# Weights streamed for a seven-product multiplication: one fetch for two products instead of one each

## The chip, the cores and the metric

The program runs on one core of one Trainium2 chip. The metric is the device time of one execution in microseconds (us). TensorE (PE) multiplies, VectorE (DVE) and ScalarE (ACT) do the elementwise work, GpSimd (POOL) and SyncE (SP) mostly start transfers. All transfers share the core's 16 DMA engines; those that SP, ACT and POOL start go through queues of their own, called q1, q10 and q0 in the profile.

## The reference

A retention layer is followed by two feed-forward layers over 3072 tokens. All arrays are float32.

```python
for t in range(S):                       # 4 batches, 8 heads, 768 steps, head width 64
    state = gamma * state + k[t] outer v[t]
    y[t] = (q[t] @ state) / 8
x = y as (3072, 512)
h = x @ moe_w_in                         # (512, 2048)
x = (h * sigmoid(1.702 * h)) @ moe_w_out # (2048, 512)
h = x @ moe2_w_in
r = maximum(h, 0)
return (r * r) @ moe2_w_out
```

## The kernel before

Every float32 factor is split into a high and a low part (hi, lo), and a product is lo·hi + hi·hi + hi·lo: three matmuls of 128x128 by 128x512 in place of one.

**Stages.** The retention layer comes first (lines 403 to 564). Then the first feed-forward layer runs on blocks 0 to 3 of 512 tokens in the plain way, with all its weights in SBUF (`up` and `down`, lines 577 to 615). While this goes on, a background program, the `maker`, builds the operands of a faster scheme out of the weights, on ACT and DVE, and writes them to DRAM through POOL and SP. The last stage, from `up2` and `down2` on, uses that scheme: a multiplication of 2x2 blocks that needs seven products instead of eight. It handles 1024 tokens at a time: one such double block of the first layer, named (0, 2), then three of the second layer, (1, 0), (1, 1) and (1, 2).

**The seven products.** `PRODUCT[i]` names the weight operand and the activation operand of product i. In `up2` a round p (0 to 7) handles one 128-row slice of each half of the hidden layer. A product there is six matmuls that read one weight operand, hi and lo together 2 KB in each of the 128 partitions, 256 KB in all. Products add up in PSUM banks X, Y and Z, and `copy` on ACT and `add` on DVE bring them into the tiles `g`. Round p runs product 1 of p, then 4 and 3 of round p-1, then 2, 6, 5 and 7 of p. In `down2` the products follow `ORDER` = 1, 2, 6, 5, 7, 4, 3, each in four slices m; one slice is twelve matmuls on two operands (p = 2m and 2m+1).

**The stream of operands.** The second stage's weights don't fit in SBUF. Each operand is a row `kw[l][m][p][i]` in DRAM (l the layer, m = 0 for up and 1 for down), 256 KB in one piece, 2 KB for each partition. `queue` lists the operands in the order of use. `fetch` starts the next transfer on SP into one of `SLOTS` = 8 places of 2 KB per partition; two of them exist early, six take the memory of the first layer's tiles `gs`, `gh` and `gl`. A transfer into a place waits until the matmuls that read its last content are through:

```python
while queue and len(fetched) < SLOTS:
    ...
    nc.sync.dma_start(out=t.bitcast(F32), in_=kw[l][m][p][PRODUCT[i][0]])
```

**What else moves data then.** At the start of round 4 of each double block `loads()` has POOL fetch the next double block's activations: four transfers `xb` of 512 KB. `background(BGUP)`, called twice a round, gives the maker 1.8 us of DVE work; one of its jobs reads 512 KB (`raw`, on ACT's queue, line 233) and writes 896 KB (`wq`, on POOL's queue, line 302, in pieces of 1 KB). The maker ends inside (1, 0). Every engine runs its instructions in the order in which the program was written; a transfer's start waits in the order of the engine that starts it.

Of the kernel before, what the change touches and what calls it, by code (L numbers as in the profile page):

```python
# [10 lines left out]
F32 = mybir.dt.float32  # L11
# [7 lines left out]
P = 128  # L19
# [18 lines left out]
QS = (11, 12, 21, 22)  # L38
PAD = 96
NSTD = 4  # L40
SLOTS = 8
EARLY = 2
BG = 4.8
BGUP = 1.8

A11, A12, A22, S1, S2, S3, S4 = range(7)
B11, B21, B22, T1, T2, T3, T4 = range(7)  # L50
PRODUCT = {1: (A11, B11), 2: (A12, B21), 3: (S4, B22), 4: (A22, T4), 5: (S1, T1), 6: (S2, T2), 7: (S3, T3)}

# [2 lines left out]
def tile_retention_then_two_ffns(  # L55
# [136 lines left out]
    def weights(f, s):  # L192
        while (f, s) not in ws:
# [5 lines left out]

    jobs = [(m, i) for m in range(2) for i in range(NJ)]  # L200

    kw = [
        [
            [dr_p.tile([7, P, 2, 256], F32, tag=f"kw{l}{m}{p}", name=f"kw{l}{m}{p}") for p in range(NQ)]
            for m in range(2)
        ]
        for l in range(2)
    ]
    made = set()
    acts = deque()  # L210

# [23 lines left out]
    def make_first():  # L235

        load(0)
        load(1)
        with tc.tile_pool(name="k1", bufs=2, side="right", reuse_waits="tile") as pool:

            def low(m, p, t, h, done):
                while not done:
                    yield None
                v.tensor_tensor(out=h[:, :, :, 1], in0=t, in1=h[:, :, :, 0], op=ALU.subtract)
                nc.gpsimd.dma_start(
                    out=kw[0][m][p][S1:S4 + 1].rearrange("i p k c -> p i (k c)"),
                    in_=h.bitcast(F32).rearrange("p i k h c -> p i (k h c)"),
                )
                made.add((0, m, p))
                yield 1.25  # L250

            last = None
            for m in range(2):
                for p in range(NQ):
                    w0, w1 = ws[p, m], ws[NQ + p, m]

                    dst = kw[0][m][p].rearrange("i p k c -> p i (k c)")
                    f0, f1 = (w.bitcast(F32).rearrange("p (j k) h c -> p j (k h c)", j=2) for w in (w0, w1))
                    if m == 0:
                        nc.sync.dma_start(out=dst[:, A11:A12 + 1], in_=f0)  # L260
                        nc.sync.dma_start(out=dst[:, A22], in_=f1[:, 1])
                    else:
                        nc.sync.dma_start(out=dst[:, A11], in_=f0[:, 0])
                        nc.sync.dma_start(out=dst[:, A12:A22 + 1], in_=f1)
                    w = pool.tile([P, 8, P], F32, tag="w", name=f"wf_{m}_{p}", bufs=1)
                    v.tensor_tensor(out=w[:, 0:4], in0=w0[:, :, 0], in1=w0[:, :, 1], op=ALU.add)
                    yield 0.7
                    v.tensor_tensor(out=w[:, 4:8], in0=w1[:, :, 0], in1=w1[:, :, 1], op=ALU.add)
                    yield 0.7
                    q0, q1, q2, q3 = (w[:, 2 * k:2 * k + 2] for k in range(4))  # L270
                    a11, a12, a21, a22 = (q0, q1, q2, q3) if m == 0 else (q0, q2, q1, q3)
                    t = pool.tile([P, 4, 2, P], F32, tag="t", name=f"wt_{m}_{p}")
                    s1, s2, s3, s4 = (t[:, k] for k in range(4))
                    v.tensor_tensor(out=s1, in0=a21, in1=a22, op=ALU.add)
                    v.tensor_tensor(out=s3, in0=a11, in1=a21, op=ALU.subtract)
                    yield 0.85
                    if last is not None:
                        yield from low(*last)
                    v.tensor_tensor(out=s2, in0=s1, in1=a11, op=ALU.subtract)
                    v.tensor_tensor(out=s4, in0=a12, in1=s2, op=ALU.subtract)  # L280
                    h = pool.tile([P, 4, 2, 2, P], F32R, tag="h", name=f"wh_{m}_{p}")
                    done = later(lambda t=t, h=h: nc.scalar.copy(out=h[:, :, :, 0], in_=t))
                    last = m, p, t, h, done
                    yield 0.85
            yield from low(*last)

    def make_second():

        with tc.tile_pool(name="k2", bufs=2, side="right", reuse_waits="tile") as pool:
# [7 lines left out]
            def low(n, w, t, done):  # L297
                while not done:
                    yield None
                m, i = jobs[n]  # L300
                v.tensor_tensor(out=t[:, :, 1], in0=w[:, 1:8], in1=t[:, :, 0], op=ALU.subtract)
                nc.gpsimd.dma_start(
                    out=kw[1][m][i // 2][:, :, i % 2].rearrange("i p c -> p i c"),
                    in_=t.bitcast(F32).rearrange("p i h c -> p i (h c)"),
                )
                if i % 2:
                    made.add((1, m, i // 2))
                yield 1.1
# [3 lines left out]
            for n in range(len(jobs)):  # L312
# [26 lines left out]
                    yield from low(*last)  # L339
                v.tensor_tensor(out=wf, in0=wf, in1=hm, op=ALU.add)  # L340
                yield 0.7
                a21, a11, a12, a22, s1, s2, s3, s4 = (w[:, k] for k in range(8))
                v.tensor_tensor(out=s1, in0=a21, in1=a22, op=ALU.add)
                v.tensor_tensor(out=s3, in0=a11, in1=a21, op=ALU.subtract)
                yield 0.6
# [54 lines left out]
    with tc.manual_schedule():  # L400
# [277 lines left out]
        for l, n in blocks:  # L678
            first, *rest = [(i, m) for i in ORDER for m in range(NQ // 2)]
            for p in range(NQ + 1):  # L680
                if p < NQ:
                    queue.append((l, n, 0, 1, p))
                else:
                    queue.extend((l, n, 1, first[0], q) for q in range(2))
                if p > 0:
                    queue.extend((l, n, 0, i, p - 1) for i in (4, 3))
                if p < NQ:
                    queue.extend((l, n, 0, i, p) for i in (2, 6, 5, 7))
            for i, m in rest:
                queue.extend((l, n, 1, i, p) for p in (2 * m, 2 * m + 1))  # L690
        fetched = {}
        turn = [0]

        def fetch():
            while queue and len(fetched) < SLOTS:
                l, n, m, i, p = key = queue[0]
                if turn[0] % SLOTS >= len(wr_p):
                    return
                assert key[:1] + key[2:3] + key[4:] in made
                queue.popleft()  # L700
                t = wr_p[turn[0] % SLOTS].tile([P, 2, 256], F32R, tag="w", name="r{}_{}_{}_{}_{}".format(*key))
                turn[0] += 1
                nc.sync.dma_start(out=t.bitcast(F32), in_=kw[l][m][p][PRODUCT[i][0]])
                fetched[key] = t

        gen = iter(())
        for n in range(NSTD):
# [50 lines left out]
        def up2(l, n, first, loads):  # L758
# [3 lines left out]

            def product(i, p, a, start):
                s, b = PRODUCT[i]
                w = fetched.pop((l, n, 0, i, p)).rearrange("p k (h c) -> p k h c", h=2)
                for k in range(2):
                    hi, lo = w[:, k, 0], w[:, k, 1]
                    matmul(a, lo, xh[b][:, k], start and k == 0, False)
                    matmul(a, hi, xh[b][:, k], False, False)
                    matmul(a, hi, xl[b][:, k], False, k == 1)  # L770
                fetch()

            def gt(q, p):
                return g[q, p // 2][:, p % 2]

            def copy(t, a):
                nc.scalar.copy(out=t, in_=a)  # L777
                while late:
                    late.popleft()()
# [8 lines left out]
            for p in range(NQ + 1):  # L788
                if p == NQ // 2:
                    loads()  # L790
                if p < NQ:
                    xb[p] = bank(f"X{l}_{n}_{p}")
                    product(1, p, xb[p][0], True)
                    copy(gt(11, p), xb[p][0])
                else:
                    next(first)
                if p > 0:
# [13 lines left out]
                    if p == NQ - 1:  # L811
                        prepare(l, n)
                if p < NQ:
                    if (l, n) != blocks[-1] and p < NQ - 1:
                        background(BGUP)
                    yb = bank(f"Y{l}_{n}_{p}")
                    product(2, p, yb[0], True)
                    add(gt(11, p), yb[0])
                    banks.append(yb[1])
                    product(6, p, xb[p][0], False)  # L820
                    copy(gt(12, p), xb[p][0])
                    zb[p] = bank(f"Z{l}_{n}_{p}")
                    product(5, p, zb[p][0], True)
                    product(7, p, xb[p][0], False)
                    copy(gt(22, p), xb[p][0])
                    add(gt(22, p), zb[p][0])
                    if (l, n) != blocks[-1] and p < NQ - 1:
                        background(BGUP)
# [46 lines left out]
        def down2(l, n, tick):  # L875
# [40 lines left out]
            for i in ORDER:  # L916
# [6 lines left out]
                for m in range(NQ // 2):  # L923
# [8 lines left out]
                    for e in range(2):  # L932
                        a = acc[e][0]
                        for p in (2 * m, 2 * m + 1):
                            w = fetched[l, n, 1, i, p].rearrange("p j (h c) -> p j h c", h=2)
                            wh, wl = w[:, e, 0], w[:, e, 1]
                            s0, s1 = p == 0 and i in (1, 2, 5), p == NQ - 1
                            matmul(a, wl, hi[:, p % 2], s0, False)
# [1 line left out]
                            matmul(a, wh, lo[:, p % 2], False, s1)  # L940
                        if m == NQ // 2 - 1:
                            after(i, e, acc)
                    for p in (2 * m, 2 * m + 1):
                        del fetched[l, n, 1, i, p]
                    fetch()
                    yield
                if i == 2:
# [105 lines left out]
```

## Time and profile before

| what | value |
|---|---|
| three timed runs | 1071.35, 1073.38, 1073.88 us (median 1073.38) |
| span of the profiled execution, first to last instruction | 1070.7 us |
| PE busy | 1049.9 us, 98% |
| DVE, ACT, POOL busy | 796.5, 511.6, 95.0 us |
| DMA | 259.34 MB, 242 GB/s |
| SP's queue q1 | 156.64 MB, 45.2% of 16 engines |
| POOL's queue q0 | 83.89 MB, 21.3% |
| fetches `r<-kw` | 448 of 256 KB, 2.9 us from start to landing (median) |

The profiled execution's own time is its span of 1070.7 us; the timed runs lie 0.6 to 3.2 us above it and their median 2.7 us. Busy shares are averages over stages with different limits, so the stages have to be looked at one by one. A matmul's busy time overlaps the next one's, so PE's idle time is the span of a stretch less its busy time.

### The profile page before, as it was taken

What the parts mean: (1) busy time and instruction counts of PE and PEld (TensorE: products, weight loads), DVE (VectorE), ACT (ScalarE), POOL (GpSimd) and SP (SyncE); (2) the same over time, 40 slices, a digit from 0 to 9 for tenths busy, and PEclk for the clock granted to TensorE, in tenths of its full rate; (3) what the DMA queues carried; (4) which work ended last, traced back from release to release, by engine and by line L of the source; (5) the groups of instructions that cost most, each with busy time, mean ns of one, the idle gap of its engine ahead of it and who ended that gap; (6) DMA issues with size and microseconds to landing.
All of it is one profiled execution on the core that took longest, in us unless ns stands there. A gap on an engine that the chain in (4) does not pass through costs nothing.

```text
span 1070.7 us, 15321 instructions
## 1 busy us (share of the span) xinstructions
PE 1049.9 (98%) x5482; PEld 870.7 (81%) x5482; DVE 796.5 (74%) x1197; ACT 511.6 (48%) x862; POOL 95.0 (9%) x143
## 2 busy tenths in 40 slices
PE   8799999999999999999999999999999999999998
PEld 6788888888888888887888887888888888888886
DVE  4988897888698889855598587889345887345953
ACT  5787554433454545454546343455233465233443
POOL 3100110111111121101000001000100000000000
PEclk9999999999999999999999999999999999999999
DMA  9997677855467685599866799766876667766664
GB/s 331 339 330 275 249 247 255 318 191 191 180 223 248 202 323 189 172 360 317 299 208 204 247 295 326 238 216 210 290 213 193 194 210 230 219 193 192 203 205 163
DMA packets 106652, 259.34 MB, mean 242 GB/s; under 512 B 11216, under 2 KB 11344, under 8 KB 106320
## 3 DMA queue, kind: packets, MB, share of 16 engines
q1 hardware_dynamic: 79088, 156.64, 45.2%
q0 software_dynamic: 22304, 83.89, 21.3%
q10 hardware_dynamic: 5184, 17.83, 5.3%
q8 instruction: 44, 0.72, 0.3%
q14 instruction: 32, 0.26, 0.1%
HBM read 184.91 MB, written 73.40 MB: 241 GB/s over the span
## 4 chain that ended last, share of the span: by engine, by line
PE 89%; DMA 6%; DVE 3%; ACT 1%; SPq 0%; issue 0%; POOL 0%; POOLq 0%; ACTq 0%
PE D L756 28%; PE X L756 15%; PE Z L756 7%; PE y L614 5%; PE h L583 5%; PE h L582 5%; PE y L613 5%; PE y L615 5%; PE h L584 5%; PE Y L756 4%; DMA r<-kw 3%; DMA unit<-qkv 3%; DVE pt L458 1%; PE sc L449 1%; PE yp L519 1%; DMA raw<-w 1%
## 5 line engine op out<-in xcount | busy, mean ns | idle before, releaser
L756 PE MATMUL D<-gx,r 128*128 128x512 f32 x1344 | 306.3, 389 | 0.0
L756 PEld LDWEIGHTS D<-gx,r 128*128 128x128 f32 x1344 | 252.0, 188 | 53.0 <-DVE gx L859 0.8
L859 DVE TENSOR_TENSOR gx<-g,gx 128x1024 fp32r<-128x1024 f32 x112 | 136.3, 1219 | 36.9 <-ACT gx L858 36.7
L858 ACT CAST gx<-g 128x1024 fp32r<-128x1024 f32 x112 | 116.6, 1051 | 93.0 <-PE D L756 83.4
L756 PE MATMUL X<-xh,r 128*128 128x512 f32 x512 | 157.9, 390 | 1.6 <-DMA r<-kw 1.6
L777 ACT COPY g<-X 128x512 f32<-128x512 f32 x96 | 56.4, 588 | 188.5 <-PE X L756 188.5
L782 DVE TENSOR_TENSOR g<-Z,g 128x512 f32<-128x512 f32 x64 | 44.2, 690 | 126.1 <-ACT g L777 93.6
L756 PEld LDWEIGHTS X<-xh,r 128*128 128x128 f32 x512 | 95.9, 188 | 22.6 <-issue 2.8
L582 PE MATMUL h<-hl,w 128*128 128x512 f32 x256 | 99.7, 389 | 0.0
L615 PE MATMUL y<-gl,w 128*128 128x512 f32 x256 | 99.6, 389 | 0.0
L756 PE MATMUL X<-xl,r 128*128 128x512 f32 x256 | 99.6, 389 | 0.0
L584 PE MATMUL h<-hl,w 128*128 128x512 f32 x256 | 99.6, 389 | 0.0
L614 PE MATMUL y<-gh,w 128*128 128x512 f32 x256 | 99.6, 389 | 0.0
L583 PE MATMUL h<-hl,w 128*128 128x512 f32 x256 | 99.6, 389 | 0.0
L613 PE MATMUL y<-gh,w 128*128 128x512 f32 x256 | 99.6, 389 | 0.0
L590 ACT CAST gh<-gs 128x512 fp32r<-128x512 f32 x64 | 39.8, 622 | 87.2 <-PE y L614 84.8
L756 PE MATMUL Z<-xh,r 128*128 128x512 f32 x256 | 79.3, 391 | 1.0 <-DMA r<-kw 0.9
L589 ACT ACTIVATE gs<-h 128x512 f32<-128x512 f32 x64 | 38.2, 597 | 64.5 <-PE h L584 51.6
L594 DVE TENSOR_TENSOR gl<-gs,gh 128x512 fp32r<-128x512 f32 x64 | 44.0, 688 | 32.0 <-ACT gh L590 32.0
L756 PEld LDWEIGHTS Z<-xh,r 128*128 128x128 f32 x256 | 47.7, 188 | 12.3 <-DMA r<-kw 2.3
L613 PEld LDWEIGHTS y<-gh,w 128*128 128x128 f32 x256 | 48.0, 188 | 10.1
L582 PEld LDWEIGHTS h<-hl,w 128*128 128x128 f32 x256 | 48.1, 188 | 10.0
(105 smaller groups left out, 1590.7 us busy)
## 6 DMA issues: line engine op xcount, KB each, us to landing
r<-kw SPq DMA_DIRECT2D x448, 256.0 KB, 2.9
kw<-wq POOLq DMA_DIRECT2D x32, 896.0 KB, 6.5
unit<-qkv SPq DMA_DIRECT2D x47, 512.0 KB, 7.5
raw<-w POOLq DMA_DIRECT2D x32, 512.0 KB, 6.0
kw<-wh POOLq DMA_DIRECT2D x16, 1024.0 KB, 4.7
kw<-w SPq DMA_DIRECT2D x16, 512.0 KB, 4.7
raw<-win ACTq DMA_DIRECT2D x16, 512.0 KB, 4.3
raw<-wout ACTq DMA_DIRECT2D x16, 512.0 KB, 4.7
```

The lines of the kernel that those rows point to most:

```text
L582: nc.tensor.matmul(hp, lo[:, k], xh, start=(k == 0), stop=False)
L583: nc.tensor.matmul(hp, hi[:, k], xh, start=False, stop=False)
L584: nc.tensor.matmul(hp, hi[:, k], xl, start=False, stop=(k == KD - 1))
L594: v.tensor_tensor(out=gl, in0=g, in1=gh, op=ALU.subtract)
L613: nc.tensor.matmul(a, lo[:, e], gh, start=s0, stop=False)
L614: nc.tensor.matmul(a, hi[:, e], gh, start=False, stop=False)
L615: nc.tensor.matmul(a, hi[:, e], gl, start=False, stop=s1)
L756: nc.tensor.matmul(a, w, b, start=start, stop=stop, skip_group_check=True)
L777: nc.scalar.copy(out=t, in_=a)
L782: v.tensor_tensor(out=t, in0=a, in1=t, op=ALU.add)
L858: nc.scalar.copy(out=hi, in_=src)
L859: v.tensor_tensor(out=lo, in0=src, in1=hi, op=ALU.subtract)
```

## The change

It does four things. Up operands of one round now lie side by side in DRAM for each partition (`kup[l][p]`, rows of 14 KB: A11, A12, A22, S4, S2, S1, S3), and down operands of two neighbouring slices likewise (`kdown[l][m]`). One fetch brings two operands, 4 KB for each partition, 512 KB in all; product 7's operand is alone, in a fetch of 256 KB. There are `SLOTS` = 4 places of 4 KB instead of eight of 2 KB. A round's products run in the order 1, 2 (both of p), 4, 3 (of p-1), 6, 5, 7, so that the products of one fetch are neighbours, and a place is given back after the second of them (2, 3, 5 or 7).

```diff
-SLOTS = 8
-EARLY = 2
+SLOTS = 4
+EARLY = 1
...
-A11, A12, A22, S1, S2, S3, S4 = range(7)
+A11, A12, A22, S4, S2, S1, S3 = range(7)
...
+    kup = [[dr_p.tile([P, 7, 512], F32, tag=f"ku{l}{p}", name=f"kup{l}{p}") for p in range(NQ)] for l in range(2)]
+    kdown = [
+        [dr_p.tile([7, P, 2, 512], F32, tag=f"kd{l}{m}", name=f"kdown{l}{m}") for m in range(NQ // 2)]
         for l in range(2)
     ]
+
+    def operands(l, m, p):
+
+        return kup[l][p] if m == 0 else kdown[l][p // 2][:, :, p % 2].rearrange("i p c -> p i c")
...
                 nc.gpsimd.dma_start(
-                    out=kw[1][m][i // 2][:, :, i % 2].rearrange("i p c -> p i c"),
+                    out=operands(1, m, i // 2)[:, :, (i % 2) * 256:(i % 2 + 1) * 256],
                     in_=t.bitcast(F32).rearrange("p i h c -> p i (h c)"),
                 )
...
                 if p < NQ:
-                    queue.append((l, n, 0, 1, p))
+                    queue.append((l, n, p, (1, 2)))
                 else:
-                    queue.extend((l, n, 1, first[0], q) for q in range(2))
+                    queue.append((l, n, *first))
                 if p > 0:
-                    queue.extend((l, n, 0, i, p - 1) for i in (4, 3))
+                    queue.append((l, n, p - 1, (4, 3)))
                 if p < NQ:
-                    queue.extend((l, n, 0, i, p) for i in (2, 6, 5, 7))
-            for i, m in rest:
-                queue.extend((l, n, 1, i, p) for p in (2 * m, 2 * m + 1))
+                    queue.extend([(l, n, p, (6, 5)), (l, n, p, (7,))])
+            queue.extend((l, n, *im) for im in rest)
...
         def fetch():
-            while queue and len(fetched) < SLOTS:
-                l, n, m, i, p = key = queue[0]
-                if turn[0] % SLOTS >= len(wr_p):
+            while queue:
+                l, n, p, q = queue[0]
+                if turn[0] % SLOTS >= len(wr_p) or turn[0] - used[0] >= SLOTS:
                     return
...
+                t = wr_p[turn[0] % SLOTS].tile([P, 2, 512], F32R, tag="w", name=f"r{turn[0]}")
                 turn[0] += 1
...
+                    nc.sync.dma_start(out=t.bitcast(F32)[:, 0:size], in_=kup[l][p][:, at:at + size])
...
+                    nc.sync.dma_start(out=t.bitcast(F32), in_=kdown[l][q][PRODUCT[p][0]])
...
-                fetch()
+                if i in (2, 3, 5, 7):
+                    used[0] += 1
+                    fetch()
...
                     copy(gt(11, p), xb[p][0])
+                    if (l, n) != blocks[-1] and p < NQ - 1:
+                        background(BGUP)
+                    yb = bank(f"Y{l}_{n}_{p}")
+                    product(2, p, yb[0], True)
+                    add(gt(11, p), yb[0])
+                    banks.append(yb[1])
                 else:
                     next(first)
...
                 if p < NQ:
-                    if (l, n) != blocks[-1] and p < NQ - 1:
-                        background(BGUP)
-                    yb = bank(f"Y{l}_{n}_{p}")
-                    product(2, p, yb[0], True)
-                    add(gt(11, p), yb[0])
-                    banks.append(yb[1])
                     product(6, p, xb[p][0], False)
```

On SP's queue, a round of the first double block. The rows are the fetches of round 2 up to the first of round 3; before, a name is r, layer, block, up or down, product, round. Before:

```order
L703 DMA r0_2_0_1_2_4556<-kw002_87 128x512
L703 DMA r0_2_0_4_1_4573<-kw001_86 128x512
L703 DMA r0_2_0_3_1_4583<-kw001_86 128x512
L703 DMA r0_2_0_2_2_4592<-kw002_87 128x512
L703 DMA r0_2_0_6_2_4610<-kw002_87 128x512
L703 DMA r0_2_0_5_2_4619<-kw002_87 128x512
L703 DMA r0_2_0_7_2_4631<-kw002_87 128x512
L703 DMA r0_2_0_1_3_4639<-kw003_88 128x512
```

Now (r7 brings products 1 and 2, r8 products 4 and 3 of round 1, r9 products 6 and 5, r10 product 7):

```order
L708 DMA r7_4558<-kup02_84 128x1024
L708 DMA r8_4574<-kup01_83 128x1024
L708 DMA r9_4593<-kup02_84 128x1024
L708 DMA r10_4601<-kup02_84 128x512
L708 DMA r11_4631<-kup03_85 128x1024
```

Seven fetches of 512 elements per partition in a round became four, three of them of 1024; r11 waits for the place of r7, the fetch of the same products one round before.

On DVE, around the start of round 5 of the first double block. `wq_25` is the maker's last operation ahead of a 896 KB write, g12 from Z is `add` after product 3, g11 from Y `add` after product 2. Before:

```order
L835 TENSOR_TENSOR g12_1_4481<-g22_1_4483,g12_1_4481 128x1024
L782 TENSOR_TENSOR g12_2_4485<-Z0_2_4_4876,g12_2_4485 128x512
L301 TENSOR_TENSOR wq_25_4851<-w32_25_4728,wq_25_4851 128x7x128
L340 TENSOR_TENSOR w32_26_4853<-w32_26_4853,hm2_26_4727 128x512
L782 TENSOR_TENSOR g11_2_4484<-Y0_2_5_4935,g11_2_4484 128x512
```

Now:

```order
L847 TENSOR_TENSOR g12_1_4459<-g22_1_4461,g12_1_4459 128x1024
L304 TENSOR_TENSOR wq_25_4781<-w32_25_4684,wq_25_4781 128x7x128
L343 TENSOR_TENSOR w32_26_4783<-w32_26_4783,hm2_26_4683 128x512
L794 TENSOR_TENSOR g11_2_4462<-Y0_2_5_4859,g11_2_4462 128x512
L794 TENSOR_TENSOR g12_2_4463<-Z0_2_4_4820,g12_2_4463 128x512
```

The maker's operation no longer stands behind the `add` of product 3, which ends two products after product 1; the write behind it can start that much earlier.

On POOL, the first writes of the second layer's up operands, five of sixteen. Before:

```order
L302 DMA kw100_101<-wq_0_3037 128x7x256
L302 DMA kw100_101<-wq_1_3090 128x7x256
L302 DMA kw101_102<-wq_2_3139 128x7x256
L302 DMA kw101_102<-wq_3_3188 128x7x256
L302 DMA kw102_103<-wq_4_3237 128x7x256
```

Now:

```order
L305 DMA kup10_90<-wq_0_3026 896x1x256
L305 DMA kup10_90<-wq_1_3079 896x1x256
L305 DMA kup11_91<-wq_2_3128 896x1x256
L305 DMA kup11_91<-wq_3_3177 896x1x256
L305 DMA kup12_92<-wq_4_3226 896x1x256
```

The pieces are 1 KB as before, but the destination is listed as 896 rows instead of 128 times 7; the writes of the down operands keep 128x7x256.

## Rows read from the trace of the kernel before

**Rows 1.** The page: busy time by engine, and the chain that ended last.

```profile
PE 1049.9 (98%) x5482; PEld 870.7 (81%) x5482; DVE 796.5 (74%) x1197; ACT 511.6 (48%) x862; POOL 95.0 (9%) x143
...
PE 89%; DMA 6%; DVE 3%; ACT 1%; SPq 0%; issue 0%; POOL 0%; POOLq 0%; ACTq 0%
```

**Rows 2.** Busy time in stretches: start:end, length, engines, PE clock, DMA share, GB/s.

```profile
0.00:108.00 108.00, 93.79 (x1275) 81.95 (x1276) 86.57 (x159) 78.68 (x251) 16.31 (x29) 0.98 0.88 317
108.00:452.40 344.40, 344.40 (x1521) 285.15 (x1520) 297.08 (x547) 164.60 (x252) 48.50 (x67) 1.00 0.66 231
...
495.00:520.00 25.00, 23.19 (x99) 18.08 (x99) 11.30 (x21) 12.56 (x23) 0.95 (x1) 1.00 0.93 341
...
655.00:670.00 15.00, 14.28 (x62) 11.20 (x62) 11.84 (x22) 5.06 (x8) 0.96 (x1) 1.00 1.02 395
...
760.00:780.00 20.00, 19.93 (x88) 16.17 (x88) 7.96 (x12) 5.10 (x9) 3.18 (x6) 1.00 0.91 323
780.00:1070.70 290.70, 286.71 (x1265) 236.89 (x1263) 181.51 (x198) 115.43 (x151) 4.34 (x8) 1.00 0.66 200
```

**Rows 3.** Waits of PE after 100 us: us in total, times, longest.

```profile
PE X L756 <- DMA r<-kw: 1.6, 3, 0.6
PE Z L756 <- DMA r<-kw: 0.9, 2, 0.7
```

**Rows 4.** The chain of waits from 484 to 512 us: start, length, what.

```profile
490.69 1.36 PE Z L756 x6
...
496.16 11.73 DMA r<-kw
507.89 0.14 issue
```

**Rows 5.** The fetches from 540 to 600 us (down2): issues, time from start to landing.

```profile
L703 SPq DMA_DIRECT2D r<-kw x45: 319/319/1493, 539.7 to 599.7; - x45
...
DMA to landing us min/median/max: 2.4/2.9/4.3
```

**Rows 6.** The fetches from 490 to 512 us.

```profile
DMA to landing us min/median/max: 3.5/9.9/11.9
```

**Rows 7.** The fetches from 640 to 670 us.

```profile
DMA to landing us min/median/max: 2.9/6.2/10.4
```

**Rows 8.** The fetches from 755 to 778 us.

```profile
DMA to landing us min/median/max: 2.5/5.0/9.5
```

**Rows 9.** The fetches from 453 to 472 us.

```profile
DMA to landing us min/median/max: 3.1/5.4/7.3
```

**Rows 10.** The fetches from 519 to 531 us.

```profile
DMA to landing us min/median/max: 2.7/4.6/6.4
```

**Rows 11.** One 512 KB load of 4 KB rows on ACT's queue, 441 to 446 us.

```profile
DMA to landing us min/median/max: 3.4/3.4/3.4
```

**Rows 12.** The four activation loads, 490 to 512 us: issues, time to landing.

```profile
L628 POOL DMA_DIRECT2D xb<-ykept x4: 528/572/636, 491.9 to 493.5; - x4
...
DMA to landing us min/median/max: 8.9/10.6/13.8
```

**Rows 13.** DMA queues from 494 to 504 us: packets, MB, share of 16 engines.

```profile
q0 software_dynamic: 700, 2.59, 71.2%
q1 hardware_dynamic: 440, 0.82, 22.1%
```

**Rows 14.** DMA queues from 655 to 663 us.

```profile
q0 software_dynamic: 491, 1.77, 55.1%
q1 hardware_dynamic: 778, 1.43, 47.7%
```

**Rows 15.** The maker's tile wq from 295 to 360 us: issues, who waited, landing.

```profile
L302 POOL DMA_DIRECT2D kw<-wq x11: 923/936/946, 299.7 to 357.7; - x11
...
  ACT wq L349: 1.2, 4
...
DMA to landing us min/median/max: 4.7/7.0/7.8
```

More of the change, by code (lines that the diff above doesn't have):

```diff
@@ L200, in tile_retention_then_two_ffns @@
     jobs = [(m, i) for m in range(2) for i in range(NJ)]
[L202 to L206, printed above, removed]
+    kup = [[dr_p.tile([P, 7, 512], F32, tag=f"ku{l}{p}", name=f"kup{l}{p}") for p in range(NQ)] for l in range(2)]
+    kdown = [
+        [dr_p.tile([7, P, 2, 512], F32, tag=f"kd{l}{m}", name=f"kdown{l}{m}") for m in range(NQ // 2)]
         for l in range(2)
     ]
+    def operands(l, m, p):
+        return kup[l][p] if m == 0 else kdown[l][p // 2][:, :, p % 2].rearrange("i p c -> p i c")
     made = set()
@@ L245, in low @@
                 nc.gpsimd.dma_start(
-                    out=kw[0][m][p][S1:S4 + 1].rearrange("i p k c -> p i (k c)"),
+                    out=operands(0, m, p)[:, S4:S3 + 1],
                     in_=h.bitcast(F32).rearrange("p i k h c -> p i (k h c)"),
@@ L255, in make_first @@
                     w0, w1 = ws[p, m], ws[NQ + p, m]
-                    dst = kw[0][m][p].rearrange("i p k c -> p i (k c)")
+                    dst = operands(0, m, p)
                     f0, f1 = (w.bitcast(F32).rearrange("p (j k) h c -> p j (k h c)", j=2) for w in (w0, w1))
@@ L272, in make_first @@
                     t = pool.tile([P, 4, 2, P], F32, tag="t", name=f"wt_{m}_{p}")
-                    s1, s2, s3, s4 = (t[:, k] for k in range(4))
+                    s4, s2, s1, s3 = (t[:, k] for k in range(4))
                     v.tensor_tensor(out=s1, in0=a21, in1=a22, op=ALU.add)
@@ L341, in make_second @@
                 yield 0.7
-                a21, a11, a12, a22, s1, s2, s3, s4 = (w[:, k] for k in range(8))
+                a21, a11, a12, a22, s4, s2, s1, s3 = (w[:, k] for k in range(8))
                 v.tensor_tensor(out=s1, in0=a21, in1=a22, op=ALU.add)
@@ L681, in tile_retention_then_two_ffns @@
                 if p < NQ:
-                    queue.append((l, n, 0, 1, p))
+                    queue.append((l, n, p, (1, 2)))
                 else:
-                    queue.extend((l, n, 1, first[0], q) for q in range(2))
+                    queue.append((l, n, *first))
                 if p > 0:
-                    queue.extend((l, n, 0, i, p - 1) for i in (4, 3))
+                    queue.append((l, n, p - 1, (4, 3)))
                 if p < NQ:
-                    queue.extend((l, n, 0, i, p) for i in (2, 6, 5, 7))
-            for i, m in rest:
-                queue.extend((l, n, 1, i, p) for p in (2 * m, 2 * m + 1))
+                    queue.extend([(l, n, p, (6, 5)), (l, n, p, (7,))])
+            queue.extend((l, n, *im) for im in rest)
         fetched = {}
-        turn = [0]
+        turn, used = [0], [0]
         def fetch():
-            while queue and len(fetched) < SLOTS:
-                l, n, m, i, p = key = queue[0]
-                if turn[0] % SLOTS >= len(wr_p):
+            while queue:
+                l, n, p, q = queue[0]
+                if turn[0] % SLOTS >= len(wr_p) or turn[0] - used[0] >= SLOTS:
                     return
-                assert key[:1] + key[2:3] + key[4:] in made
                 queue.popleft()
-                t = wr_p[turn[0] % SLOTS].tile([P, 2, 256], F32R, tag="w", name="r{}_{}_{}_{}_{}".format(*key))
+                t = wr_p[turn[0] % SLOTS].tile([P, 2, 512], F32R, tag="w", name=f"r{turn[0]}")
                 turn[0] += 1
-                nc.sync.dma_start(out=t.bitcast(F32), in_=kw[l][m][p][PRODUCT[i][0]])
-                fetched[key] = t
+                if isinstance(q, tuple):
+                    assert (l, 0, p) in made
+                    at, size = PRODUCT[q[0]][0], len(q)
+                    assert all(PRODUCT[i][0] == at + j for j, i in enumerate(q))
+                    nc.sync.dma_start(out=t.bitcast(F32)[:, 0:size], in_=kup[l][p][:, at:at + size])
+                    for j, i in enumerate(q):
+                        fetched[l, n, 0, i, p] = t[:, j]
+                else:
+                    assert (l, 1, 2 * q) in made and (l, 1, 2 * q + 1) in made
+                    nc.sync.dma_start(out=t.bitcast(F32), in_=kdown[l][q][PRODUCT[p][0]])
+                    fetched[l, n, 1, p, q] = t
         gen = iter(())
@@ L764, in product @@
                 s, b = PRODUCT[i]
-                w = fetched.pop((l, n, 0, i, p)).rearrange("p k (h c) -> p k h c", h=2)
+                w = fetched.pop((l, n, 0, i, p)).rearrange("p (k h c) -> p k h c", k=2, h=2)
                 for k in range(2):
@@ L934, in down2 @@
                         for p in (2 * m, 2 * m + 1):
-                            w = fetched[l, n, 1, i, p].rearrange("p j (h c) -> p j h c", h=2)
+                            w = fetched[l, n, 1, i, m][:, p % 2].rearrange("p (j h c) -> p j h c", j=2, h=2)
                             wh, wl = w[:, e, 0], w[:, e, 1]
@@ L942, in down2 @@
                             after(i, e, acc)
-                    for p in (2 * m, 2 * m + 1):
-                        del fetched[l, n, 1, i, p]
+                    del fetched[l, n, 1, i, m]
+                    used[0] += 1
                     fetch()
```

## The prediction

> **What bounds the kernel now.** I read the page's busy times first. PE is busy 98% of the span and makes 89% of the chain that ended last [rows 1], so time can only come from, or go into, PE's idle time. The table of stretches says where that lies [rows 2]: 108.00 - 93.79 = 14.2 us in the first 108 us (the retention layer, untouched by the change), none from 108 to 452.4 us, 1.81 us from 495 to 520, 0.72 from 655 to 670, 0.07 from 760 to 780, and 290.70 - 286.71 = 4.0 us at the end, where the last sums are stored. Together 20.8 us, which is 1070.7 - 1049.9. PE's own waits name the cause of the three in the middle: after 100 us it waits for nothing but fetches of operands, 1.6 + 0.9 = 2.5 us [rows 3], 2.6 us by the stretches. So all that a better stream can give back is 2.6 us, 0.24%. About 0.3% (3.2 us) is what a measurement of this kernel can tell from no change.
>
> The question is then how near the stream is to not keeping up. One product is 1.36 us of PE [rows 4], so it eats 256 KB per 1.36 us, 193 GB/s. A fetch lands in 2.9 us where little else moves [rows 5]. The chain of waits shows a fetch started at 496.16 us that landed after 11.73 us, and PE waiting for it [rows 4]. Around it the fetches need up to 11.9 us [rows 6]; up to 10.4 in the next double block [rows 7] and 9.5 in the one after [rows 8]. All three follow the four `xb` loads of 512 KB (started from 491.9 to 493.5 us in the first of them, landing after 8.9 to 13.8 us [rows 12]). The last double block loads no next activations and has no such burst.
>
> **What the change removes.** Fewer fetches start, 4 instead of 7 in a round of up products, one instead of two in a down slice. SP's starts of 319 ns [rows 5] are far from filling 1.36 us, so this is worth nothing by itself; what hides it is the stretch in which a fetch lies started and PE is at earlier products.
>
> **What it takes away: cover.** Before, the fetch for product k starts when product k-8 is through: seven products lie between, 7 x 1.36 = 9.5 us. Now a place is freed after the second product of a pair, and the pair that comes into it four fetches later must be there whole for its first product. Between 1, 2 of one round and 1, 2 of the next lie 4, 3, 6, 5, 7: five products, 6.8 us; the same five for pairs 4, 3 and 6, 5; six, 8.2 us, for 7 alone. In the down slices three slices of 2.72 us lie between, 8.2 us, before as now (two places were freed together there). Also, the 512 KB take longer: a load of that size in 4 KB rows on a queue of the same kind took 3.4 us [rows 11]. What is left for being late was 9.5 - 2.9 = 6.6 us and is now 6.8 - 3.4 = 3.4 us.
>
> **The sum, upper bound.** Take the lateness of a fetch (its longest landing less 2.9) as it was: 9.0, 7.5 and 6.6 us in the three bursts. Against 6.6 us of cover that leaves 2.4, 0.9 and 0: 3.3 us, of which PE in fact waited 2.6, because a waiting PE asks for nothing while the queue clears; a factor 0.8. Against 3.4 us it leaves 5.6, 4.1 and 3.2. Two smaller bursts, the maker's reads and writes in the first double block, were hidden and now show: 7.3 - 2.9 - 3.4 = 1.0 us [rows 9] and 6.4 - 2.9 - 3.4 = 0.1 us [rows 10]. Sum 14.0, times 0.8 = 11.2; less today's 2.6 it is +8.6 us.
>
> **Lower bound.** Rows of 4 KB may move more bytes at each turn of SP's queue. From 494 to 504 us q1 moved 0.82 MB in 440 packets beside 2.59 MB in 700 of q0 [rows 13]: 82 of 341 GB/s, where PE eats 193, so 1.11 MB were missed in 10 us. At the same turns with double rows q1 gets 1.64 against 2.59, 39% or 132 GB/s; q0's 2.59 MB then last 12.4 us, and 12.4 x (193 - 132) = 0.76 MB are missed, 0.68 of 1.11. Lateness 6.1, 5.1 and 4.5 less 3.4 leaves 2.7 + 1.7 + 1.1 = 5.5, times 0.8 = 4.4; the small bursts (4.4 x 0.68 = 3.0) stay hidden. Less 2.6 it is +1.8 us.
>
> Which end? In the second burst q1 already had more packets than q0, 778 against 491, and 1.43 MB in 8 us, 179 GB/s [rows 14], nearly what PE eats; its fetches were late all the same, up to 10.4 us [rows 7]. Lateness there is not a matter of q1's share of the bytes alone, and that speaks for the end that leaves it as it is. I take two thirds of the way up: +6 us.
>
> **The rest at nothing, and its cover.** The new order lets the maker's operations on DVE start without product 3's `add` ahead of them, up to two products (2.7 us) earlier, and with them the 896 KB write on POOL and the `raw` load on ACT. They then fall closer to the `xb` loads, which stand on POOL's queue between them; I give this no value, but keep 2.5 us for the top of the range. PSUM and the copies: product 6 follows product 1 after three others as before, product 4 of a round follows product 7 after two instead of one, so ACT gets more time (a copy is behind PE today without a wait of PE [rows 3]). At the start of the stream, product 6's pair goes where the last `gh` of an even f lay; that is free 2.72 us before 452.4, and needed two products after it: 5.4 us against 3.4. The fourth fetch waits until 452.4 and is needed five products later, 6.8 us, with up to 7.3 us of landing around it [rows 9]; that is in the 1.0 us above. No such bound exists for the writes of the maker from 108 to 452 us, where PE has no idle time [rows 2] because ACT and DVE run ahead; they are a rival below.
>
> Sum: 1070.7 + 6.0 = 1076.7 us of span. The median of the timed runs lies 2.7 us above this execution's span, so **1079.4 us**.
>
> **Rivals.**
>
> *A. The longer rows get the stream its share, and it is no slower.* If q1 gets 48% of the bytes in a burst instead of 24%, (193 - 0.48 x 341) GB/s over 2.59 MB / (0.52 x 341) = 14.6 us is 0.43 MB, and 9.0 us of lateness falls to 3.5, the new cover. From that share on all waits end: 1073.4 - 2.6 = 1070.8 us, and shares in between give up to 1076.6. For it: both kinds of transfer are then 512 KB in 4 KB rows, so equal turns mean 50%. Against: the trace's 440 and 700 packets [rows 13] and 778 and 491 [rows 14] are no equal turns.
> The Trainium skill, page "DMA: Bandwidth & Descriptors", section "Queues, rings and completion order", says that an engine takes a whole packet of some 9 to 17 descriptors from one queue before it turns to the next. By that rule both would get half and A would hold, an estimate of 1070.8 us; but it would have given q1 a third of the bytes from 494 to 504 us, and the trace shows 24% [rows 13].
>
> *B. The writes of the up operands get slower.* They are now 896 rows. Eleven of them start in 58 us, 5.8 us apart, land after 7.0 us, and ACT's cast of `wq`, which needs the tile of two jobs before, already waits for them, 1.2 us in 4 times [rows 15]. Above some 7.8 us each further us holds a job by half a us; behind the waiting cast stand the first layer's casts, and PE behind these. At 10 us: 16 x 1.5 = 24 us, 1103 us with the rest. Against it: pieces of 1 KB and the bytes are as before.
>
> *C. Faster by over 0.3%.* More than the 2.6 us there are would have to go; no row shows where. The most that the stream can give is in A.
>
> **How the numbers follow.** Lost cover, between +1.8 and +8.6: 0.68, of which 0.05 below +3.2. A: 0.24. B: 0.05. C: 0.03. So slower by over 0.3% 0.63 + 0.05 = 0.68, within 0.3% 0.24 + 0.05 = 0.29, faster 0.03. The top is 1073.4 + 8.6 + 2.5 = 1084.5. At the bottom 1073.5 leaves out the better part of A, some 0.10, and C; B lies above the top.
>
> **What would show it.** Right: PE's waits for r in the up stages grow from 2.6 to some 9 us, most in the three stretches after the `xb` loads, none in the down stages; fetches of 512 KB land in some 3.4 us in quiet and in over 6.8 us where PE waits; from 108 to 452 us PE stays without idle time. A holds if the longest landing falls below 7 us and q1 has half the bytes in the burst. B holds if PE has idle time before 452 us and ACT waits for the writes. The prediction is wrong if lateness depends on the number of fetches that are under way (up to eight before, four now) more than on the bytes ahead of them: then fewer and larger ones are less late, and the sum's upper half falls away.

## The result and the profile after

The changed kernel takes 1077.38 us (median of 8 runs, 1075.11 to 1082.83) beside 1073.51 us for the kernel before (8 runs, 1067.66 to 1075.05). The ratio is 1.0054, with a 95% interval of 1.0031 to 1.0076: slower by 5.8 us (3.3 to 8.2). The ratio goes by all runs and not by the two medians, which lie 3.9 us apart.

The page of the profiled execution (span 1074.4 us), as [rows 1]:

```profile
PE 1049.4 (98%) x5482; PEld 870.5 (81%) x5482; DVE 796.0 (74%) x1197; ACT 511.6 (48%) x862; POOL 93.2 (9%) x143
...
PE 88%; DMA 7%; issue 2%; ACT 1%; SPq 0%; POOL 0%; DVE 0%; POOLq 0%; ACTq 0%
```

PE's waits from 100 us to the end, as [rows 3]; the last three numbers are us in total, times, longest:

```profile
PE X L766 <- DMA r<-kup: 6.3, 4, 2.4
```

2.5 us in five waits became 6.3 us in four. The stretches, as [rows 2], show where, and one thing more: the clock column of 502.40:505.60.

```profile
108.00:450.00 342.00, 342.00 (x1511) 283.09 (x1510) 294.82 (x543) 162.62 (x249) 46.14 (x66) 1.00 0.65 231
495.00:501.40 6.40, 3.93 (x17) 2.62 (x16) 4.88 (x7) 3.00 (x5) 0.00 (x0) 1.00 1.01 403
502.40:505.60 3.20, 3.20 (x9) 2.53 (x8) 0.00 (x0) 0.60 (x1) 0.14 (x1) 0.50 1.02 376
520.00:536.00 16.00, 14.79 (x66) 11.95 (x65) 9.85 (x11) 8.19 (x13) 1.01 (x1) 1.00 0.89 301
655.00:665.00 10.00, 8.38 (x37) 6.64 (x36) 8.65 (x14) 3.69 (x6) 0.99 (x1) 1.00 1.03 408
760.00:785.00 25.00, 23.92 (x106) 19.51 (x105) 8.57 (x13) 5.36 (x9) 3.19 (x6) 1.00 0.82 281
```

Idle are 2.47, 1.21, 1.62 and 1.08 us: after each of the three groups of activation loads, and once more at the end of the first up stage. Before 450 us nothing is idle. The chain of waits from 490 to 540 us, as [rows 4]:

```profile
491.75 9.44 DMA r<-kup
...
501.32 2.03 PE X L766 x6
503.35 2.54 PE Z L766 x6
...
525.29 7.85 DMA r<-kup
...
533.27 1.63 PE X L766 x6
```

The pair that was started at 491.75 landed after 9.44 us, 2.4 us late, and the two products behind it took 2.03 and 2.54 us instead of 1.36: the granted clock was 0.50, 1.2 GHz, for some 3.2 us. That is 2.03 + 2.54 - 2.72 = 1.85 us on top of the wait. Not all of it is the clock's: the first product behind the wait of 525.29 us took 1.63 us at full clock, 0.27 more than 1.36, so the low clock cost some 1.6 us, which is also half of 3.2. The fetches behind which PE waited in the next two double blocks, from the chain of the whole program:

```profile
653.38 8.26 DMA r<-kup
...
766.98 7.71 DMA r<-kup
```

The fetches' times to landing in 485 to 515, 640 to 675 and 755 to 790 us and, quiet, in 540 to 600 us, as [rows 5 to 8]:

```profile
DMA to landing us min/median/max: 3.4/6.7/10.5
...
DMA to landing us min/median/max: 3.5/4.4/8.8
...
DMA to landing us min/median/max: 2.7/3.9/7.8
...
DMA to landing us min/median/max: 3.1/4.2/5.8
```

The long landings became a little shorter (11.9, 10.4 and 9.5 before), and still PE waits longer. In all three bursts the longest is that of product 7's operand alone, 256 KB, which has six products until its use; the pairs that PE waited for landed after 9.44, 8.26 and 7.71 us. From the chain of the whole program, the first product of each up stage and the long piece of each down stage. Before:

```profile
452.61 1.36 PE X L756 x6
...
534.27 73.57 PE D L756 x324
607.85 1.36 PE X L756 x6
...
688.00 73.57 PE D L756 x324
761.58 1.36 PE X L756 x6
...
840.82 73.57 PE D L756 x324
914.39 1.36 PE X L756 x6
...
993.27 73.45 PE D L756 x324
```

After:

```profile
450.77 1.36 PE X L766 x6
...
536.26 73.57 PE D L766 x324
609.83 1.36 PE X L766 x6
...
690.62 73.61 PE D L766 x324
764.23 1.36 PE X L766 x6
...
844.47 73.61 PE D L766 x324
918.07 1.36 PE X L766 x6
...
996.95 73.45 PE D L766 x324
```

The up stages took 81.66, 80.15, 79.24 and 78.88 us and take 85.49, 80.79, 80.24 and 78.88: 5.5 us more together. The down stages are the same. In the two executions that were profiled the streamed part happens to begin 1.8 us earlier after the change (its start lay between 447.7 and 453.8 us in the profiles of the kernels below, too), so the spans differ by 3.7 us only; the 5.5 us of the up stages agree with the 5.8 of the timed runs. They are, but for 0.1 us, 6.3 - 2.5 = 3.8 us of waits and 1.6 us of low clock. The timed runs point to the clock too: its mean over an execution is 0.993 in the eight of the changed kernel and 0.996 in those of the kernel before that stand beside the experiments below.

### The profile page after: what moved, and what is told of

It reads as the page before. It is cut to its first block, busy times and chain, and to the rows that moved or that the text cites. A ratio compares the mean times of both kernels' runs of the same rounds, so it can differ in the third digit from the quotient of the medians.

```text
span 1074.4 us, 14884 instructions
## 1 busy us (share of the span) xinstructions
PE 1049.4 (98%) x5482; PEld 870.5 (81%) x5482; DVE 796.0 (74%) x1197; ACT 511.6 (48%) x862; POOL 93.2 (9%) x143
## 4 chain that ended last, share of the span: by engine, by line
PE 88%; DMA 7%; issue 2%; ACT 1%; SPq 0%; POOL 0%; DVE 0%; POOLq 0%; ACTq 0%
PE D L766 28%; PE X L766 15%; PE Z L766 8%; PE h L587 5%; PE y L618 5%; PE h L585 5%; PE y L616 5%; PE y L617 5%; PE h L586 5%; PE Y L766 4%; DMA r<-kup 3%; DMA unit<-qkv 3%; DMA raw<-w 1%; ACT vs L476 1%; PE yp L522 1%
## 5 line engine op out<-in xcount | busy, mean ns | idle before, releaser
L766 PEld LDWEIGHTS X<-xl,r 128*128 128x128 f32 x256 | 48.2, 188 | 10.1
```

The costliest lines, as they stand in the source:

```text
L766: nc.tensor.matmul(a, w, b, start=start, stop=stop, skip_group_check=True)
```

## The experiments

Theory: the stream lost cover, and each burst of other transfers that outlasts what is left makes PE wait. Rivals: the new order moves the maker's transfers onto the activation loads; pairs are bad in themselves; longer rows change the stream's share. "Waits" are PE's waits for fetches after 108 us, read from one execution of each kernel; ratios are to the kernel before, run on the same chip, over all runs. The execution read was the fastest of ten for the new order alone (1067.15 us), for seven places (1071.10) and for the loads on SP's queue (1068.18), so of two kernels a microsecond of waits tells less than the ratios.

**The new order alone.**

```diff
-                    queue.append((l, n, 0, 1, p))
+                    queue.extend((l, n, 0, i, p) for i in (1, 2))
...
-                    queue.extend((l, n, 0, i, p) for i in (2, 6, 5, 7))
+                    queue.extend((l, n, 0, i, p) for i in (6, 5, 7))
...
+                    if (l, n) != blocks[-1] and p < NQ - 1:
+                        background(BGUP)
+                    yb = bank(f"Y{l}_{n}_{p}")
+                    product(2, p, yb[0], True)
...
-                    product(2, p, yb[0], True)
...
```

> The kernel before with the new order of the up products (1, 2, 4, 3, 6, 5, 7) alone: eight places of 2 KB, one fetch for each product. Lost cover: seven products still lie between a fetch's start and its use (9.5 us), so PE waits for fetches 2 to 4 us as before (2.5) and the time is within 0.3% of before, 1071 to 1076 us. Rival, the order does the harm (the maker's writes and reads start earlier and fall onto the activation loads): the waits rise to 5 us or more and the time to 1076 to 1079 us.

Measured 1071.62 us beside 1071.88, ratio 0.9989 (0.9970 to 1.0008), waits 2.0 us. The order costs nothing.

**The maker's calls put back.**

```diff
                     copy(gt(11, p), xb[p][0])
-                    if (l, n) != blocks[-1] and p < NQ - 1:
-                        background(BGUP)
                     yb = bank(f"Y{l}_{n}_{p}")
...
                 if p < NQ:
+                    if (l, n) != blocks[-1] and p < NQ - 1:
+                        background(BGUP)
                     product(6, p, xb[p][0], False)
```

> The changed kernel with the first background call of a round put back behind the add of product 3, as in the kernel before, so that the maker's write and read no longer start earlier; pairs, places and product order stay. Lost cover: waits of 5 to 7.5 us (6.3 in the changed kernel), time within 0.3% of the changed kernel. Rival, the maker's earlier transfers are a good part of the loss: waits of at most 4.5 us and a time of 1073 to 1075 us.

1077.8 us, ratio 1.0062 (1.0035 to 1.0088), waits 5.3 us. The loss stays: the maker's earlier transfers are not its cause.

**Six and seven places, nothing else changed.**

```diff
-SLOTS = 8
+SLOTS = 6
```

> The kernel before with six places instead of eight: old layout, old order, fetches of 256 KB, five products (6.8 us) between a fetch's start and its use, as in the changed kernel, and two slices (5.4 us) in the down stages. Lost cover: the waits rise from 2.5 us to 5 to 9 us, in the same three stretches after the activation loads, and the time to 1076 to 1081 us, with neither pairs nor long rows. Rival, the pairs themselves (one landing for two products, 512 KB each) do the harm: the waits stay under 4 us and the time at 1071 to 1076 us.

1082.24 us beside 1071.88, ratio 1.0095 (1.0078 to 1.0112). PE's waits:

```profile
PE Z L756 <- DMA r<-kw: 4.4, 2, 3.2
PE Y L756 <- DMA r<-kw: 3.8, 3, 3.2
PE X L756 <- DMA r<-kw: 1.1, 2, 0.7
```

9.3 us, with fetches of 256 KB: fewer places alone do the harm. With `SLOTS = 7`:

> The kernel before with seven places instead of eight: six products (8.2 us) between a fetch's start and its use. Lost cover: between the 2.5 us of waits with eight places and the 9.3 us with six, that is 4 to 7 us, and a time 0.2 to 0.7% over before. Rival, a threshold elsewhere (six places are too few for the down slices, say): waits as with eight, under 3.5 us, and no change of time.

1077.1 us beside 1070.89, ratio 1.0049 (1.0030 to 1.0069).

```profile
PE Y L756 <- DMA r<-kw: 3.3, 2, 2.0
PE X L756 <- DMA r<-kw: 2.0, 3, 1.1
PE Z L756 <- DMA r<-kw: 0.7, 2, 0.5
```

6.0 us: eight, seven and six places give 2.5, 6.0 and 9.3 us of waits. Seven single places come out like the changed kernel (6.3 us, 1.0054), six do not. The execution with 6.0 us of waits took 1071.10 us at a clock of 1.000, six us less than the median; the other nine had 0.993 to 0.997, so what they lost holds low clock beside the waits.

**Two transfers of 256 KB into each place.**

```diff
-                    nc.sync.dma_start(out=t.bitcast(F32)[:, 0:size], in_=kup[l][p][:, at:at + size])
+                    for j in range(size):
+                        nc.sync.dma_start(out=t.bitcast(F32)[:, j], in_=kup[l][p][:, at + j])
...
-                    nc.sync.dma_start(out=t.bitcast(F32), in_=kdown[l][q][PRODUCT[p][0]])
+                    for j in range(2):
+                        nc.sync.dma_start(out=t.bitcast(F32)[:, j], in_=kdown[l][q][PRODUCT[p][0]][:, j])
```

> The changed kernel with two transfers of 256 KB (rows of 2 KB) into each place instead of one of 512 KB: places, order and cover stay. Lost cover: the waits stay at 5 to 7.5 us (6.3 in the changed kernel), a little less where the first half lands earlier; time within 0.3% of the changed kernel. Rival, rows of 4 KB give the stream a larger share of the DMA engines in a burst: without them the waits rise to 9 to 11 us, the end of the sum at which lateness stays as it was, and the time to 1080 to 1083 us.

1077.12 us beside 1071.88, ratio 1.0049 (1.0034 to 1.0064).

```profile
PE X L768 <- DMA r<-kup: 5.4, 4, 2.6
PE Z L768 <- DMA r<-kup: 0.6, 2, 0.4
```

6.0 us. For the time, transfers of 512 KB in rows of 4 KB can't be told from 256 KB in rows of 2 KB, though the rows did change the landings (with halves the fetches that PE waited for landed after 11.32, 9.43 and 9.87 us, with pairs after 9.44, 8.26 and 7.71) and the share of the bytes. The queues from 492 to 502 us, the changed kernel:

```profile
q0 software_dynamic: 693, 2.61, 66.9%
q1 hardware_dynamic: 364, 1.29, 33.0%
```

and the one with halves:

```profile
q0 software_dynamic: 699, 2.62, 72.9%
q1 hardware_dynamic: 523, 0.96, 26.1%
```

1.29 MB of 3.90 (33%) against 0.96 of 3.66 (26%).

**Places that are always full.** In the changed kernel three places hold pairs and one product 7's operand alone: seven operands, as with seven single places. Here any two neighbours share a place.

```diff
+                if turn[0] % SLOTS >= len(wr_p) or turn[0] - used[0] // 2 >= SLOTS:
+                    return
...
+                for j in range(2):
+                    l, n, m, i, p = key = queue.popleft()
+                    assert (l, m, p) in made
+                    nc.sync.dma_start(out=t.bitcast(F32)[:, j], in_=operands(l, m, p)[:, PRODUCT[i][0]])
+                    fetched[key] = t[:, j]
```

> The changed kernel with four places of 4 KB that hold any two operands which follow each other in use, by two transfers of 256 KB: product 7's place no longer stands half empty, so eight operands are held where the changed kernel holds seven (three pairs and one alone). Between the start of a fetch and the first use of its operands lie six products (five in the changed kernel). Operands held decide: as with eight single places, waits of 2.5 to 4 us and a time within 0.3% of before. Products up to the first use decide: as with seven single places, where six lay between too, waits of 5 to 7 us and 0.3 to 0.7% over before.

1073.06 us beside 1072.03, ratio 1.0002 (0.9980 to 1.0023).

```profile
PE X L759 <- DMA r<-kup: 2.1, 4, 0.9
PE Z L759 <- DMA r<-kup: 1.7, 3, 1.0
PE Y L759 <- DMA r<-kup: 0.3, 1, 0.3
```

4.1 us, just above what the operands held were to give, and the time is that of before: its interval lies below that of the kernel with halves, which moves the same transfers but leaves half a place empty. The loss went with the empty half place.

**Activation loads one a round.** Both kernels got the same edit.

```diff
+LOADS = (4, 5, 6, 7)
...
-                if p == NQ // 2:
+                if p in LOADS:
                     loads()
...
+                if parts:
+                    parts.popleft()()
```

In the changed kernel:

> The changed kernel with the four activation loads of 512 KB started one in each of rounds 4 to 7 instead of all at the start of round 4. Lost cover: it is lost only where a burst is longer than it, so the waits for fetches fall from 6.3 us to under 2, and the time to 1069 to 1073 us, with the smaller cover untouched. Rival, the pairs or the smaller place count cost something at every burst of the maker too: the waits stay at 4 us or more, above all in the first double block, and the time at 1075 us or more.

1081.36 us, ratio 1.0092 (1.0075 to 1.0108). The theory's numbers missed and the rival's were met: waits grew.

```profile
PE X L777 <- DMA r<-kup: 9.8, 7, 2.4
```

The DMA issues from 682 to 692 us show why (count, KB, us to landing):

```profile
kdown<-wq POOLq DMA_DIRECT2D x1, 896.0 KB, 6.1
xb<-ykept POOLq DMA_DIRECT2D x1, 512.0 KB, 8.0
r<-kup SPq DMA_DIRECT2D x1, 512.0 KB, 8.2
```

On POOL's queue the loads stand behind maker's writes that wait for ACT or DVE, and start right behind them: in the first two double blocks two behind one write and one behind each of two more (the last such couple starts at 682.1 and 683.1 us). The fetches that PE waited for landed after 7.2 to 9.0 us, over the 6.8 us until their first use. One long burst became several that are each long enough. In the third double block no maker's write holds POOL back, and all four loads started together at 770.6 us, near the start of the up stage, as they do without the edit (765.8). Whether the pairs or the smaller reserve are at fault, the same edit in the kernel before tells:

> The kernel before (nine and a half us of cover) with the four activation loads started one in each of rounds 4 to 7. In the changed kernel the same edit made the waits grow to 9.8 us, since every pair of a maker's write and one load delays a fetch by some 8.3 us. Lost cover: 8.3 is over 6.8 but under 9.5, so here the waits fall from 2.5 us to under 0.5, and the time by 1 to 3 us (1069 to 1073 beside a before of 1072 to 1073). Rival, spreading itself is bad, whatever the cover: waits of 4 us or more here too.

1066.61 us beside 1071.89, ratio 0.9946 (0.9927 to 0.9964), and no waits at all. The gain, 5.8 us (3.9 to 7.8), is more than was expected and more than the 2.5 us of waits that were there. PE's busy time from 452 to 1062 us is the stretch, but for 0.16 us:

```profile
452.00:1062.00 610.00, 609.84 (x2688) 503.68 (x2686) 412.16 (x492) 268.05 (x360) 29.89 (x48) 1.00 0.74 238
```

The same edit takes 2.5 us of waits to none with eight places, and 6.3 to 9.8 with the changed kernel's four. This version beats both kernels. In the profiled executions the streamed part, from its first product to the end, takes 1065.8 - 451.9 = 613.9 us beside 1070.7 - 452.6 = 618.1, 4.2 less: the five waits and, behind each, a first product that takes some 0.27 us longer make 3.9. The rest of the 5.8 stays open.

**Loads at the end of the up stage.**

```diff
-                if p == NQ // 2:
+                if p == NQ:
                     loads()
```

In the changed kernel:

> The changed kernel with all four activation loads started at the end of the up stage (round 8) instead of round 4, so that most of the fetches that they delay belong to the down stage, with 8.2 us of cover instead of 6.8, and few of the maker's transfers fall on them. Lost cover: the waits fall from 6.3 us to 1 to 4, and the time to 1070 to 1075 us, within 0.3% of before. Rival, fetches by pairs are late in any burst: the waits stay at 6 us or more and move into the down stages.

1079.55 us, ratio 1.0068 (1.0043 to 1.0093), waits 7.0 us: a miss. The waits are as long as the rival had them. In the first two double blocks PE waited 2.2 and 2.5 us for the last pair of the up stage, which landed after 8.9 and 9.1 us; the down stage itself had no waits, so the rival's place was wrong. In the third the edit moved nothing: POOL had nothing to wait for and started the loads at 768.3 us (765.8 in the changed kernel), and PE waited 2.0 us there. In the kernel before:

> The kernel before with the same late start of the activation loads. Lost cover: cover is 9.5 us in the up stage and 8.2 in the down stage, so fetches of 9 to 10 us show there a little: waits of 0 to 2 us (2.5 before), time 1069 to 1073 us, the same as before or a little less. Rival, cover doesn't decide, the place of the burst does: the waits are the same as those of the changed kernel with late loads, within 1 us.

1070.98 us, ratio 0.9987 (0.9969 to 1.0005), waits 1.2 us, 5.8 less than in the changed kernel.

**Loads one a round on SP's queue.** Changed kernel, with `nc.sync.dma_start` for the spread loads instead of `nc.gpsimd.dma_start`.

> The changed kernel with the activation loads started one in each of rounds 4 to 7, as in the spread kernel, but on SP's queue among the fetches instead of on POOL's queue behind the maker's write, so that no 896 KB write and 512 KB load start together. A fetch behind a load then lands about 3.4 + 1.3 us after its start in quiet and some 6.5 beside a write. Lost cover: under 6.8 us, so the waits fall from 9.8 us (spread on POOL) and 6.3 (unspread) to at most 3, and the time to within 0.3% of before or below. Rival, pairs of 512 KB in four places are too coarse for any other transfer: waits of 5 us or more and a time 0.4% or more over before.

1071.98 us beside 1070.89, ratio 1.0012 (0.9992 to 1.0031), waits 1.9 us, all in the first double block. On SP's queue the loads of the third double block are spread as well (793.7 to 822.3 us). Once the loads are taken apart in all three, the changed kernel's places nearly suffice, and its loss can't be told from nothing.

## Why the prediction was right, and where it was not

**The direction and the place held.** PE waits more, after the activation loads, and not in the down stages; the time is 2 us under the forecast and inside its range. What the argument rested on, a stream whose reserve is shorter than its bursts, is shown from both sides: taking places away from the kernel before gives the loss (six, seven places), and filling the places (eight operands) or taking the burst apart (loads on SP's queue) takes it away.

**The size was right by luck: two errors offset each other.** The sum had 8.6 us of waits after the change, 6 more than before; 6.3 us were measured, 3.8 more. Nothing in it stood for the clock, which cost some 1.6 us.

**The term that was too large is lateness.** The sum took it two thirds of the way up from the lower bound. The pairs that PE waited for after the loads landed after 9.44, 8.26 and 7.71 us. Less 3.4 that is 6.0, 4.9 and 4.3 us, 0.65 to 0.67 of the 9.0, 7.5 and 6.6 before: the lower bound's 0.68. The queue's share of the bytes, 33%, lies between the 24% of before and that bound's 39%, and with rows of 2 KB in the same places the landings stay long, so longer rows did make fetches less late. The number under way did not: with seven and six single fetches the first burst's longest landing was 11.6 and 11.5 us beside 11.9. What had spoken for the upper end, the second burst, showed the same fall. Over 6.8 us of cover the three landings leave 2.6 + 1.5 + 0.9 = 5.0 us, and PE was idle for 2.47 + 1.62 + 1.08 = 5.2: for the changed kernel the count of cover came out, and without the factor 0.8.

**The count of cover doesn't carry over to all runs as it stands.** It takes the longest landing of each burst, subtracts the products up to the first use and multiplies the sum by 0.8. For the other kernels, with the loads where they were:

| kernel | longest landings, us | up to the first use, us | waits by the count, us | measured in all, us |
|---|---|---|---|---|
| seven single places | 11.6, 9.7, 10.0 | 8.2 | 5.4 | 6.0 |
| six single places | 11.5, 10.7, 8.5 | 6.8 | 8.2 | 9.3 |
| two transfers into each place | 11.9, 9.6, 9.9 | 6.8 | 8.8 | 6.0 |
| places that are always full | 13.3, 10.2, 9.5 | 8.2 | 6.7 | 4.1 |

It comes near for single places and is too high where two transfers fill one. With one product more, as a place's second operand has, it gives 5.4 and 3.6. With the halves PE did wait for second operands in the second and third burst (the fetches of 9.43 and 9.87 us, for products into bank Z); for the rest this is argued only. The number of operands that the places hold orders the runs too, in waits and in time: eight 2.0 to 4.1 us and ratios up to 1.0002 (the kernel before, the new order alone, four full places), seven 5.3 to 6.3 and 1.0049 to 1.0062 (seven places, the changed kernel, with halves, with the maker's calls put back), six 9.3 and 1.0095. More operands held are also more products up to their uses, so these runs don't tell the two accounts apart. By both, the harm is not that two products share a fetch but that product 7's place stands half empty, and filling it took the loss away. That PE lives off whatever is under way until it is used up would explain such an order, but is argued only. The 2.0 to 4.1 us among eight leave room for a small cost of freeing by twos; their ratios don't tell them apart.

**The ceiling was too low.** The prediction held 2.6 us, 0.24%, for all that a better stream can give back. The kernel before with its loads one a round gave 5.8 us (3.9 to 7.8): a wait costs more than its idle time, here some 0.27 us more for the product behind it, which accounts for a part.

**The smaller bursts.** 1.1 us was put on them, near 460 and 525 us. The first showed no wait; at the second PE waited 1.2 us, for the fetch of 525.29 us.

**Rival A fell.** The longer rows got the stream 33% of the bytes, from 24% [rows 13], not the 48% from which waits end, and taking them away left the time as it was (halves). By the rule of the Trainium skill that A named ("DMA: Bandwidth & Descriptors", "Queues, rings and completion order") it would have been half; the traces show a third.

**Rival B fell.** PE has no idle time from 108 to 450 us, and the up operands' writes land after 6.9 us (median) as against 7.0 [rows 15]. Its price was mis-summed besides: by its own rule, half of what lies above 7.8 us, a landing of 10 us costs 1.1 us a job and 16 x 1.1 = 18 us, not 24.

**The 2.5 us kept for the maker's earlier transfers** were not needed: putting them back gave 1.0062.

## What to carry to other kernels

Count a stream's reserve in operands held, or in products up to each operand's use, not in bytes of SBUF: a coarser place that some operand fills only by half is a place lost, and one of eight cost 0.5% here. Compare the longest landing in the trace, not the median, with the time to use; where a burst sets it, look in the trace at when the transfers start and which queue's order makes them start together. Taking the burst apart on POOL's queue paid (0.54%) only in the kernel whose reserve outlasted each part; on SP's queue, where the loads did come one at a time, it took the other kernel's loss away.

## What had not been expected of the hardware

A short wait can cost more than itself: after 2.47 us without work in 495 to 501.4 us PE's granted clock was at 1.2 GHz for the stretch from 502.4 to 505.6 us, and two products cost 1.85 us more, some 1.6 of them by the clock. It doesn't follow from the length of a wait alone. With six places, after PE had stood still from 500 to 503 us the clock stayed at 2.4 GHz, and in the next double block, after a wait of 3.16 us, it went down to 1.2 GHz for 6.8 us. The stretches of that kernel:

```profile
500.00:503.00 3.00, 0.02 (x1) 0.00 (x0) 1.58 (x2) 0.83 (x2) 0.00 (x0) 1.00 1.04 415
503.00:510.00 7.00, 5.64 (x22) 4.08 (x23) 2.90 (x4) 0.70 (x2) 0.95 (x1) 1.00 1.05 399
...
661.80:668.60 6.80, 5.53 (x13) 4.37 (x14) 3.34 (x5) 0.00 (x1) 0.96 (x1) 0.50 1.03 378
```
